# Moving the sum of the rest ahead of the last pieces of w2, and cutting those pieces 7 + 2

## The chip, the cores and the metric

The kernel runs on one core of a Trainium2 chip. The metric is the device time of one execution in microseconds (us), lower is better. Most numbers below come from profiled executions; one such trace covers the span from the first to the last instruction, about 1.8 us less than the device time.

## The reference, cut to what matters

```python
xn = _layernorm(x)                       # x: (2, 1, 576)
return x + attention(xn) @ wo + mlp(xn)

# attention: 32 query heads, 16 kv heads, the last 2048 positions of an 8192-long cache
# mlp: h = relu(xn @ w1 + b1) ** 2 ; out = h @ w2 + b2     w2: (4608, 576)
```

Only two tokens are decoded. The work is therefore reading 53.6 MB of caches and weights once; the weight w2 comes last.

## The kernel before

`D` is 576, `OH` is `D/2`, `OQ` is `D/4`, `B` is 2, `FR` is 9. The rows of w2 come in four groups of nine per partition (one tile each); the last group is cut in two transfers, so there are five pieces. All sums but those of the last group accumulate in `out_ps`, as two halves of 288 columns at partitions 0 and 32. The last group uses another accumulator, `tail_ps`, with four column groups of 144 columns at partitions 0, 32, 64 and 96. What has gathered in `out_ps` ("the sum of the rest") is copied to SBUF and added into `tail_ps` by four f32 matmuls with an identity, between the two last pieces.

```python
    W2P = [(0, 0, 9), (1, 0, 9), (2, 0, 9), (3, 0, 6), (3, 6, 9)]   # group, first row, end row

    def mlp_tail(r0, r1):
        w2_sb = w2_tiles.pop((NG4 - 1, r0))
        if r0 == 0:
            mlp["out"] = psum.tile([P, OQ], F32, tag="misc", name="tail_ps")
        for r in range(r0, r1):
            o = (r - r0) * D
            for i in range(4):
                pe_mm(mlp["out"][32 * i:32 * i + B, :], lhsT=mlp["h"][:, (NG4 - 1) * FR + r, :],
                                 rhs=w2_sb[:, o + i * OQ:o + (i + 1) * OQ], start=(r == 0), stop=(r == FR - 1),
                                 skip_group_check=True, tile_position=(0, 32 * i))
    # ... all of attention ...
    for w in W2P[1:NG4 - 1]:
        mlp_o(*w)                        # second and third piece of w2, into out_ps
    for i in range(2):
        nc.vector.tensor_copy(out=part[:, i * OH:(i + 1) * OH], in_=out_ps[32 * i:32 * i + B, :])
    mlp_tail(*W2P[NG4 - 1][1:])          # 6 rows
    for i in range(4):                   # the sum of the rest
        pe_mm(mlp["out"][32 * i:32 * i + B, :], lhsT=ident_f[0:B, 0:B], rhs=part[:, i * OQ:(i + 1) * OQ],
              start=False, stop=False, skip_group_check=True, tile_position=(0, 32 * i))
    mlp_tail(*W2P[NG4][1:])              # 3 rows

    for i, (cp, eng) in enumerate(((nc.vector.tensor_copy, nc.sync), (nc.scalar.copy, nc.scalar))):
        fin_sb = work.tile([B, OH], BF16, tag="fin", name=f"fin_sb_{i}")
        for q in range(2):
            k = 2 * i + q
            cp(out=fin_sb[:, q * OQ:(q + 1) * OQ], in_=mlp["out"][32 * k:32 * k + B, :])
        eng.dma_start(out=out2d[:, i * OH:(i + 1) * OH], in_=fin_sb[:])
```

## Time and profile before

| what | value |
|---|---|
| device time, three runs | 133.96, 134.13, 134.67 us; median 134.13 |
| span of the trace | 132.3 us |
| main transfer queue | 53.61 MB, 95.0% of its 16 engines' span |
| busiest compute engine | TensorE, 67% |
| third piece of w2 starts on TensorE | 126.07 us |
| last piece of w2 starts on TensorE | 129.17 us |
| final casts start | 129.55 us (VectorE) |

The lines behind this table are shown in the prediction below. They are to be read from the end backwards: find what the last instruction waited for, and go on until something waits for nothing but a transfer. From 126.07 to 129.55 is the only stretch that the change touches. I call those 3.48 us "the interval" throughout: from the start of the third piece's matmuls to the start of VectorE's first final cast.

### The profile page before, as it was taken

Reading aid. Unit: us, or ns where it says so; the run is one execution under the profiler, and the core shown is the slowest. Engines: PE = TensorE matmul, PEld = TensorE weight load, DVE = VectorE, ACT = ScalarE, POOL = GpSimd, SP = SyncE. Lnnn points to the kernel's source line nnn. Section 1 sums busy time; section 2 is a strip of 40 time slices with the busy share of each in tenths; the row PEclk is TensorE's granted clock in tenths of the full one; section 3 lists DMA queues with packets and bytes.
Section 4 is the critical chain, followed back from the end, with each engine's and each line's share of the span. In section 5 each row is a group of like instructions: output and inputs, shape, how many; then the busy total and the mean of one; then the engine's idle time right before and its main releaser. Section 6 shows DMA issues by size and latency. Waiting matters only on the chain.

```text
span 132.3 us, 2040 instructions
## 1 busy us (share of the span) xinstructions
PE 89.0 (67%) x830; PEld 54.4 (41%) x830; DVE 59.6 (45%) x151; ACT 43.9 (33%) x63; POOL 7.7 (6%) x26
## 2 busy tenths in 40 slices
PE   0069319689862957699479989389703996499761
PEld 0059202629521355466174466064403661155430
DVE  6944400224640018555915685827730458644021
ACT  2716400015710136737236447145300651200001
POOL 7700000001000001010010010000010000000000
PEclk9999995955999599999968999977975699869999
DMA  4999989999998999999999999999999999999950
GB/s 139 394 461 468 423 381 431 436 466 514 414 401 352 436 416 451 416 446 426 426 431 426 436 421 443 416 435 431 432 436 426 431 433 439 411 420 429 421 230 1
DMA packets 3632, 53.74 MB, mean 406 GB/s; under 512 B 412, under 2 KB 420, under 8 KB 680
## 3 DMA queue, kind: packets, MB, share of 16 engines
q1 hardware_dynamic: 3604, 53.61, 95.0%
q8 instruction: 6, 0.10, 0.3%
q10 hardware_dynamic: 20, 0.01, 0.0%
q14 instruction: 2, 0.02, 0.0%
HBM read 53.62 MB, written 0.00 MB: 405 GB/s over the span
## 4 chain that ended last, share of the span: by engine, by line
DMA 70%; PE 22%; DVE 2%; ACT 2%; issue 1%; SPq 1%; DVEq 0%; ACTq 0%
DMA k<-in_A_k_cache_dram 42%; DMA w<-in_B_w_dram 14%; DMA wq_sb<-in_A_wq_dram 13%; PE kT_ps L86 11%; PE sc_ps L83 4%; PE q_ps L83 3%; PE pv_ps L83 2%; PE qs_ps L83 1%; DVE kT L286 1%; ACT kT L284 1%; ACT pr L323 1%; PE sm L83 1%; DVE qrow L250 1%; SPq L105 0%; DVE qz L266 0%
## 5 line engine op out<-in xcount | busy, mean ns | idle before, releaser
L86 PE MATMUL kT_ps<-ident_f,k 128*128 128x128 f32 x256 | 41.1, 317 | 12.4 <-DMA k<-in_A_k_cache_dram 11.8
L284 ACT COPY kT<-kT_ps 128x1024 bf16<-128x1024 bf16 x32 | 31.9, 1011 | 36.0 <-PE kT_ps L86 35.7
L86 PEld LDWEIGHTS kT_ps<-ident_f,k 128*128 128x128 f32 x256 | 34.0, 164 | 21.7 <-issue 18.2
L286 DVE COPY kT<-kT_ps 128x1024 bf16<-128x1024 bf16 x32 | 22.1, 691 | 31.5 <-PE kT_ps L86 31.4
L83 PE MATMUL sc_ps<-kT,qz 128*32 128x512 bf16 x128 | 10.5, 414 | 4.6 <-DVE kT L286 2.8
L83 PE MATMUL pv_ps<-v,pT 128*32 128x512 bf16 x128 | 11.9, 440 | 1.0 <-DVE acc L358 0.8
L312 POOL PARTITION_ALL_REDUCE gmax<-m x8 | 2.9, 366 | 103.1 <-DVE m L310 103.1
L323 ACT ACTIVATE pr<-sc_ps,nb 128x512 bf16<-128x512 f32 x8 | 5.5, 687 | 8.3 <-DVE nb L320 8.3
L83 PEld LDWEIGHTS <-xnT 128*4 128x4 bf16 x90 | 3.0, 110 | 12.0 <-issue 11.6
L83 PE MATMUL q_ps<-wq_sb,xnT 128*4 128x512 bf16 x36 | 3.8, 603 | 4.7 <-DMA wq_sb<-in_A_wq_dram 4.7
L308 DVE TENSOR_REDUCE mx<-sc_ps 128x1 f32<-128x512 f32 x8 | 5.5, 683 | 3.1 <-PE sc_ps L83 3.1
L83 PEld LDWEIGHTS <-qz 128*32 128x32 bf16 x128 | 2.3, 98 | 10.1 <-DVE kT L286 6.2
L83 PE MATMUL h_ps<-w_sb,xnT 128*4 128x384 bf16 x54 | 4.1, 443 | 3.2 <-DMA w_sb<-in_B_w_dram 3.2
L358 DVE SCALAR_TENSOR_TENSOR mix<-pv_ps,own_j,mix 128x128 f32<-128x128 f32 x16 | 5.6, 351 | 0.6
L564 ACT CAST fin_sb<-tail_ps 2x144 bf16<-2x144 f32 x2 | 0.5, 272 | 15.8 <-PE tail_ps L83 15.8
L329 DVE STREAM_TRANSPOSE pT<-pr 128x512 bf16<-128x512 bf16 x8 | 5.6, 703 | 0.2 <-ACT pr L323 0.2
L86 PE MATMUL pro_ps<-ident,xs 2*128 2x2 bf16 x10 | 0.6, 165 | 7.6 <-DVE xs L180 7.6
L83 PEld LDWEIGHTS <-pT 128*32 128x32 bf16 x128 | 2.9, 99 | 6.1 <-issue 3.7
L83 PE MATMUL out_ps<-wo_sb,ws 128*2 128x288 bf16 x64 | 5.0, 318 | 0.3 <-DVE ws L387 0.3
L83 PE MATMUL sm<-acc,tohead 128*64 128x129 f32 x16 | 3.7, 315 | 1.8 <-DVE acc L358 1.8
L83 PE MATMUL out_ps<-w,hT_sb 128*2 128x288 bf16 x54 | 3.8, 286 | 1.3 <-DMA w<-in_B_w_dram 1.3
L431 DVE TENSOR_TENSOR hs<-hT_ps,hodd 128x20 f32<-128x20 f32 (+1 forms) x4 | 0.5, 172 | 9.2 <-ACT hodd L428 9.2
(77 smaller groups left out, 58.2 us busy)
## 6 DMA issues: line engine op xcount, KB each, us to landing
k<-in_A_k_cache_dram SPq DMA_DIRECT2D x8, 2048.0 KB, 7.7
v<-in_A_v_cache_dram SPq DMA_DIRECT2D x8, 2048.0 KB, 18.1
w_sb<-in_B_w_dram SPq DMA_DIRECT2D x1, 5184.0 KB, 19.1
wq_sb<-in_A_wq_dram SPq DMA_DIRECT2D x1, 4608.0 KB
wo_sb<-in_A_wo_dram SPq DMA_DIRECT2D x2, 2304.0 KB
w<-in_B_w_dram SPq DMA_DIRECT2D x3, 1296.0 KB, 25.7
w<-in_B_w_dram SPq DMA_DIRECT2D x1, 864.0 KB
w<-in_B_w_dram SPq DMA_DIRECT2D x1, 432.0 KB
```

Source lines behind the costliest of these rows:

```text
L83: return tc.keep_in_program_order(nc.tensor.matmul(out, **kw))
L86: return tc.keep_in_program_order(nc.tensor.transpose(**kw))
L250: nc.vector.tensor_copy(out=qrow[:, 0, :], in_=q_ps[0][0:RB, :])
L284: pin(nc.scalar.copy(out=dst, in_=src))
L286: pin(nc.vector.tensor_copy(out=dst, in_=src))
L308: pin(nc.vector.tensor_reduce(out=mx[:], in_=sc_ps, axis=AX.X, op=ALU.max))
L312: nc.gpsimd.partition_all_reduce(gmax[:], m2[:], channels=P, reduce_op=ReduceOp.max)
L323: pin(nc.scalar.activation(out=pr[:], in_=sc_ps, func=ACT.Exp, bias=nb[:], scale=scale, accum_out=acc[:, Dh:Dh + 1]))
L329: pin(nc.vector.transpose(out=pT[:].rearrange("p t m -> p (t m)"), in_=pr[:]))
L358: op = nc.vector.scalar_tensor_tensor(out=nx, in0=pv_ps[:, j, :], scalar=own_j[:, j:j + 1], in1=acc, op0=ALU.mult, op1=ALU.add)
L431: nc.vector.tensor_tensor(out=hs[:].rearrange("p (g r) b -> p r g b", g=NG4)[:, r0:r0 + n, g:g + 2, :], in0=even[:, :, g:g + 2, :], in1=od ...
L564: cp(out=fin_sb[:, q * OQ:(q + 1) * OQ], in_=mlp["out"][32 * k:32 * k + B, :])
```

## The change

The intent is to shorten what TensorE has to do once the last bytes are there. The sum of the rest enters first and opens the accumulators, its two copies run side by side on VectorE and ScalarE, and the last group of w2 is cut so that only two rows, eight matmuls, come behind the last landing.

```diff
@@ mlp_tail
-        if r0 == 0:
-            mlp["out"] = psum.tile([P, OQ], F32, tag="misc", name="tail_ps")
...
-                                 rhs=..., start=(r == 0), stop=(r == FR - 1),
+                                 rhs=..., start=False, stop=(r == FR - 1),
@@
-    W2P = [(0, 0, 9), (1, 0, 9), (2, 0, 9), (3, 0, 6), (3, 6, 9)]
+    W2P = [(0, 0, 9), (1, 0, 9), (2, 0, 9), (3, 0, 7), (3, 7, 9)]
@@
-    for i in range(2):
-        nc.vector.tensor_copy(out=part[:, i * OH:(i + 1) * OH], in_=out_ps[32 * i:32 * i + B, :])
-    mlp_tail(*W2P[NG4 - 1][1:])
+    for i, cp in enumerate((nc.vector.tensor_copy, nc.scalar.copy)):
+        cp(out=part[:, i * OH:(i + 1) * OH], in_=out_ps[32 * i:32 * i + B, :])
+    mlp["out"] = psum.tile([P, OQ], F32, tag="misc", name="tail_ps")
     for i in range(4):
         pe_mm(mlp["out"][32 * i:32 * i + B, :], lhsT=ident_f[0:B, 0:B], rhs=part[:, i * OQ:(i + 1) * OQ],
-              start=False, stop=False, skip_group_check=True, tile_position=(0, 32 * i))
+              start=True, stop=False, skip_group_check=True, tile_position=(0, 32 * i))
+    mlp_tail(*W2P[NG4 - 1][1:])
     mlp_tail(*W2P[NG4][1:])
```

More of the change, by code (lines that the diff above doesn't have):

```diff
@@ L452, in mlp_tail @@
                 pe_mm(mlp["out"][32 * i:32 * i + B, :], lhsT=mlp["h"][:, (NG4 - 1) * FR + r, :],
-                                 rhs=w2_sb[:, o + i * OQ:o + (i + 1) * OQ], start=(r == 0), stop=(r == FR - 1),
+                                 rhs=w2_sb[:, o + i * OQ:o + (i + 1) * OQ], start=False, stop=(r == FR - 1),
                                  skip_group_check=True, tile_position=(0, 32 * i))
```

## The prediction

> **What bounds the kernel now.** I read the page first for the overall balance, then the chain that ended last, then the last microseconds in order of time, then short windows of the transfer rate.
>
> The page of the kernel before has the busy shares, the slices of the DMA engines and the sum for the queue:
>
> ```profile
> PE 89.0 (67%) x830; PEld 54.4 (41%) x830; DVE 59.6 (45%) x151; ACT 43.9 (33%) x63; POOL 7.7 (6%) x26
> DMA  4999989999998999999999999999999999999950
> q1 hardware_dynamic: 3604, 53.61, 95.0%
> ```
>
> The reader is to see that no compute engine is above 67% of the span, while the main DMA queue fills 95.0% of what its 16 engines could work, at 90% or more in nearly every slice. The program is a stream of 53.61 MB, and an order of instructions can only matter where the stream has ended and something still follows it. So everything that this change can do lies after about 126 us of a span of 132.3 us.
>
> The chain that ended last, asked for its final 30 us (start, length, what):
>
> ```profile
> 110.00 19.13 DMA w<-in_B_w_dram
> 129.13 0.04 issue
> 129.17 0.46 PE tail_ps L83 x12
> 129.63 0.04 ACT fin_sb L564
> ```
>
> The last transfer of w2 lands at 129.13, and from there the chain goes through the twelve matmuls of the last three rows (3 rows x 4 column groups), then the two casts and the output. The four matmuls that add the sum of the rest are not on the chain, nor is its copy by VectorE.
>
> The order of time for the same stretch (start, length, engine, line, operation, and in brackets the idle time before it and what ended it):
>
> ```profile
> 126.07 1.27 PE L83 MATMUL out_ps<-w,hT_sb 128*2 128x288 bf16 x18 [1.32 <-DMA w<-in_B_w_dram]
> 127.37 0.93 DVE L553 COPY part<-out_ps 2x288 f32<-2x288 f32 x2 [5.90 <-PE out_ps L83]
> 128.13 0.55 PE L83 MATMUL tail_ps<-w,hT_sb 128*2 128x144 bf16 x24 [0.80 <-DMA w<-in_B_w_dram]
> 128.60 0.42 PE L83 MATMUL tail_ps<-part,ident_f 2*2 2x144 f32 x8
> 129.17 0.36 PE L83 MATMUL tail_ps<-w,hT_sb 128*2 128x144 bf16 x12
> 129.55 0.62 DVE L564 CAST fin_sb<-tail_ps 2x144 bf16<-2x144 f32 x2 [1.26 <-PE tail_ps L83]
> 129.62 0.57 ACT L564 CAST fin_sb<-tail_ps 2x144 bf16<-2x144 f32 x2 [15.78 <-PE tail_ps L83]
> ```
>
> Three arrivals show as starts of TensorE: the third piece of w2 at 126.07, the 6-row piece at 128.13, the 3-row piece at 129.17. Six rows took 128.13 - 126.07 = 2.06 us, which is 0.34 us a row; three rows took 129.17 - 128.13 = 1.04 us, which is 0.35 us a row. So the arrivals are paced by the rate of the transfer alone. The part that the change wants out of the way, the f32 matmuls, ran from 128.60 to 129.02 and was over 0.11 us before the last piece had landed (129.13). This is the decisive reading: that work is already hidden, though by a thin margin.
>
> Windows of the last stretch (window; length, then busy time of PE, PEld, DVE, ACT, POOL; clock; DMA share; GB/s):
>
> ```profile
> 126.00:126.50 0.50, 0.43 (x8) 0.33 (x9) 0.00 (x0) 0.00 (x0) 0.00 (x0) 1.00 0.97 380
> 127.50:128.00 0.50, 0.00 (x0) 0.00 (x0) 0.47 (x2) 0.00 (x0) 0.00 (x0) 1.00 0.39 159
> 128.50:129.00 0.50, 0.50 (x20) 0.15 (x9) 0.00 (x0) 0.00 (x0) 0.00 (x0) 1.00 0.06 21
> 129.00:129.50 0.50, 0.36 (x16) 0.19 (x12) 0.00 (x0) 0.00 (x0) 0.00 (x0) 1.00 0.00 0
> ```
>
> The DMA share falls from 0.97 to 0.39 and 0.06 before the last landing: most of the 16 engines have run dry and a few late ones finish. The granted clock is 1.00 in all four windows, so the throttle needs no account here.
>
> **What the Trainium skill says.** "DMA: Bandwidth & Descriptors", section "Why a DMA increments its semaphore by 16 and not by 1", says that the engines of one transfer finish independently and that only the full count of 16 means that all its data has landed. The trace agrees: the tail of the share shows stragglers, and TensorE starts its last group only after 129.13. What decides is therefore how many bytes the slowest engine has to move in total, and a new cut of the same last nine rows does not change that.
>
> "TensorE: Matmul & The Clock Gate", Part 3, section "The mechanism", has matmuls on different tiles of the array overlapping, so that each further one adds only its start offset. The trace agrees in kind: one matmul of a row and column group lasts 225 ns, yet 24 of them span 0.55 us and 12 span 0.36 us, an offset of (0.55 - 0.225)/23 = 14 ns and (0.36 - 0.225)/11 = 12 ns. The page's own offset of about 4 ns is not what is seen here; I use 12 to 14.
>
> "VectorE: DVE Perf Modes", in the section on the TRN2 errata, gives a copy from PSUM to SBUF as 120 cycles plus one per element at 0.96 GHz for VectorE and 172 plus one per element at 1.2 GHz for ScalarE. For 288 elements on VectorE that is 425 ns against 447 in the trace; for 144 elements on ScalarE it is 263 ns against 272. For the new ScalarE copy of 288 elements I take the traced 272 ns plus 144/1.2 = 120 ns: an estimate of 0.39 us.
>
> "PSUM — Partial Sum Buffer", section "PSUM bank collisions raise a hardware error", asks that two engines on one bank be kept apart by bank and quadrant of 32 partitions. The two halves of the sum lie at partitions 0 and 32, so they may be copied at once. In the trace the two final casts do just that on one buffer, from 129.55 to 130.17 and from 129.62 to 130.19.
>
> **The change part by part.** In order of time, with the duration of each from the rows above:
>
> The copy. Before, two VectorE copies of 447 ns one after the other, 127.37 to 128.30. After, one on each engine: VectorE from 127.37 to 127.82, ScalarE from about 127.4 to 127.83 (estimate of 0.39 us and a start 0.04 to 0.07 us later, as in the final casts). The sum is ready at about 127.83 instead of 128.30: 0.47 us earlier. None of it was on the path.
>
> The f32 matmuls. The same eight rows of the trace (four matmuls of two passes each), 0.42 us. They move from 128.60 to about 127.88 and end at 128.30, in a stretch where TensorE sat idle for 0.80 us waiting for data. They open the accumulators now. Worth to the end: nothing, as they were over before 129.13 anyway.
>
> The first of the two pieces has 7 rows. It should land one row later, at 128.13 + 0.35 = 128.48, which is after the f32 matmuls' end by 0.18 us. Its 28 matmuls take 0.225 + 27 x 0.014 = 0.60 us, to 129.08; TensorE has started the last of them at 128.86, so it is free when the last piece lands.
>
> The last piece has 2 rows. It ends at the same total of bytes, so it should land at 129.13 as before. Eight matmuls follow instead of twelve: 0.225 + 7 x 0.012 = 0.31 us instead of 0.36. This is the only term on the path: 4 x 12 to 14 ns, about 0.05 us.
>
> What follows is untouched: two casts on each engine (0.62 and 0.57 us) and the output of 1.1 KB on each of two queues. The instruction order of the other engines is the same in both builds up to this point; only ScalarE gains one copy and VectorE loses one.
>
> Sum: 0.00 (copy) + 0.00 (f32 matmuls) + 0.00 (landing) - 0.05 (four matmuls fewer) = -0.05 us, and 134.13 - 0.05 = 134.08. That is 0.04%.
>
> **The rivals.** First, TensorE rather than the transfer could be what holds the last group. For it: between the end of the f32 matmuls (129.02) and the start of the last group (129.17) lie only 0.15 us, so in an execution where the stragglers come earlier, the f32 matmuls would be on the path. Against it: the chain names the landing at 129.13, and three rows in 1.04 us fit the rate of the six rows before. If it were so, the change would gain up to 0.15 us more, and give about 133.9.
>
> Second, the smaller last piece could move less efficiently: a row of it is 2 x 1152 = 2304 bytes a partition instead of 3456. For it: smaller packets may cost more a byte. Against it: a line through the two arrivals (2.06 us for six rows, 1.04 us for three) leaves 0.02 us for a piece on its own, and there are two pieces of 128 rows in both kernels, so what the smaller piece loses the larger wins back. If it cost 0.1 us, the result would be 134.2.
>
> Third, the new order makes TensorE take the f32 matmuls before the 7-row piece, so a late ScalarE copy would hold that piece back. For it: ScalarE had been idle for 15.78 us before its final cast, and the matmuls of its half wait for it. Against it: the sum would be ready 0.65 us before the 7-row piece lands, less the 0.42 us of f32 matmuls; after using up those 0.18 us of slack it would have to eat another 129.13 - 128.86 = 0.27 us before the last group suffered. It would take a copy of over 0.8 us. I expect no cost; if it happened, 134.3.
>
> Fourth, and largest in size: the scatter of the stream itself. The three runs of before lie at 133.96, 134.13 and 134.67, a spread of 0.71 us, more than ten times the effect. A median of a few runs of the changed kernel can fall on either side of 134.13 for that reason alone.
>
> **The range and the chances.** The middle is 134.08, shaded to 134.06 because the first rival can only gain. Downward, the first rival's 0.15 us and a median that falls 0.2 us low give about 133.7; upward, the scatter seen between the middle and the highest run (0.54 us) counts in part, which gives 134.45. Two per cent is 2.68 us. The whole stretch from the landing of the third piece to the end is 132.3 - 126.07 = 6.2 us, and 3.1 us of it are waiting for bytes that both kernels move; I see no way to gain or lose 2.68 us there. So within 2% gets 0.98.
>
> **What would show each step right or wrong.** Right: in the order of time, one part copy on each engine side by side, ending at about 127.8 when counted on this trace's scale; the eight f32 rows begin within 0.1 us of it and end before the 7-row piece starts TensorE; that piece is 2.4 us behind the third piece, the 2-row piece 0.7 us behind it; the last group spans about 0.31 us; the chain still goes from the transfer of w2 through eight matmuls to the casts. The interval from the third piece's start to the start of the casts is 129.55 - 126.07 = 3.48 us before and should be 3.43 after. Wrong: if that interval shrinks by over 0.15 us, TensorE and not the transfer was binding; if the 2-row piece comes over 3.2 us after the third piece, cutting has a cost; if the 28 matmuls have not started when the last piece lands, the copy has become the wait. A span that moves by more than 0.3 us with this interval unchanged would be the stream before 126 us, not the change.

## The result, and the profile after

The changed kernel takes 134.01 us in the median of six runs (133.95 to 134.37), against 134.11 us for six runs of the kernel before. The ratio is 0.9992, with a 95% interval from 0.9972 to 1.0013: the same. Ratios here are the mean time of one kernel's fast runs over that of the other's of the same rounds, so they are not quite the ratio of the medians that I quote.

The page of the kernel after, the lines that answer to those of before:

```profile
PE 89.0 (67%) x830; PEld 54.7 (41%) x830; DVE 59.1 (45%) x150; ACT 44.2 (33%) x64; POOL 7.7 (6%) x26
DMA  4999989999998999999999999999999999999950
q1 hardware_dynamic: 3604, 53.61, 95.2%
```

VectorE (DVE) has one instruction fewer and ScalarE (ACT) one more; the stream is the same.

The chain that ended last, its end (start, length, what):

```profile
109.99 19.10 DMA w<-in_B_w_dram
129.09 0.04 issue
129.13 0.40 PE tail_ps L83 x8
129.53 0.05 ACT fin_sb L563
```

It goes through the same transfer as before. Behind it stand eight matmuls and 0.40 us to the casts instead of twelve and 0.46 us.

The same stretch in order of time (start, length, engine, line, operation; in brackets the idle time before and what ended it):

```profile
126.00 1.27 PE L83 MATMUL out_ps<-w,hT_sb 128*2 128x288 bf16 x18 [1.15 <-DMA w<-in_B_w_dram]
127.30 0.45 DVE L551 COPY part<-out_ps 2x288 f32<-2x288 f32 x1 [5.73 <-PE out_ps L83]
127.33 0.39 ACT L551 COPY part<-out_ps 2x288 f32<-2x288 f32 x1 [13.50 <-PE out_ps L83]
127.80 0.42 PE L83 MATMUL tail_ps<-part,ident_f 2*2 2x144 f32 x8 [0.54 <-DVE part L551]
128.43 1.00 PE L83 MATMUL tail_ps<-w,hT_sb 128*2 128x144 bf16 x36 [0.20 <-DMA w<-in_B_w_dram]
129.46 0.63 DVE L563 CAST fin_sb<-tail_ps 2x144 bf16<-2x144 f32 x2 [1.71 <-PE tail_ps L83]
```

The copies lie side by side, the f32 matmuls end at 128.22, and TensorE still waits 0.20 us for the 7-row piece at 128.43. This view merges both pieces into one line of 36 matmuls; the chain gives the start of the last eight as 129.13. The interval is 129.46 - 126.00 = 3.46 us, against 3.48 before.

The windows of the last stretch (window; length, busy time of PE, PEld, DVE, ACT, POOL; clock; share of the DMA engines; GB/s):

```profile
127.50:128.00 0.50, 0.20 (x8) 0.10 (x8) 0.25 (x1) 0.22 (x1) 0.00 (x0) 1.00 0.39 154
128.50:129.00 0.50, 0.50 (x28) 0.38 (x28) 0.00 (x0) 0.00 (x0) 0.00 (x0) 1.00 0.03 9
129.00:129.50 0.50, 0.33 (x12) 0.10 (x7) 0.04 (x1) 0.00 (x0) 0.00 (x0) 1.00 0.00 0
```

The f32 matmuls (x8) now run in a window in which TensorE was wholly idle before, while the share of the transfers falls away just as it did.

### The profile page after: what moved, and what is told of

Same layout as the page of the kernel before. It is cut to its first block, busy times and chain, and to the rows that moved or that the text cites. A ratio compares the mean times of both kernels' runs of the same rounds, so it can differ in the third digit from the quotient of the medians.

```text
span 132.2 us, 2040 instructions
## 1 busy us (share of the span) xinstructions
PE 89.0 (67%) x830; PEld 54.7 (41%) x830; DVE 59.1 (45%) x150; ACT 44.2 (33%) x64; POOL 7.7 (6%) x26
## 4 chain that ended last, share of the span: by engine, by line
DMA 72%; PE 20%; DVE 2%; ACT 2%; issue 1%; SPq 1%; DVEq 0%; ACTq 0%
DMA k<-in_A_k_cache_dram 44%; DMA w<-in_B_w_dram 14%; DMA wq_sb<-in_A_wq_dram 13%; PE kT_ps L86 10%; PE sc_ps L83 4%; PE q_ps L83 3%; PE pv_ps L83 2%; PE qs_ps L83 1%; DVE kT L286 1%; ACT kT L284 1%; ACT pr L323 1%; PE sm L83 1%; DVE qrow L250 1%; SPq L105 0%; DVE qz L266 0%
```

## The experiments

Every kernel was run six times and traced in one of those runs. The theory: the last landing of w2 sets the end ("landing theory"), the sum of the rest was hidden already, and only matmuls behind the landing count. The main rivals: TensorE and its f32 matmuls held the last group; cutting has a cost; the copy takes the place of the wait.

One thing about the runs has to be said first, because it changes how they must be compared. The 50 runs of the kernel before that were made beside these experiments fall into two groups with nothing between: 34 runs from 133.91 to 134.29 us, mean 134.09, and 16 runs from 134.54 to 134.77 us, mean 134.65. Both count as fast, so the medians and ratios mix them. I call them the lower and the upper group, and compare like with like where I can.

| kernel | median us | its six runs, us | ratio to before | interval us | clock in the tail of the trace |
|---|---|---|---|---|---|
| before | 134.13 | (50 runs, above) | | 3.48 | 1.00 |
| after | 134.01 | 133.95 to 134.37 | 0.9992 | 3.46 | 1.00 |
| after, again | 134.07 | 133.93 to 134.24 | 0.9991 | 3.46 | 1.00 |
| order only | 134.70 | 134.08, 134.21, then 134.69 to 134.82 | 1.0015 | 4.13 | 0.50 |
| cut only | 134.29 | 134.26 to 134.36, and 135.19 | 1.0008 | 3.64 | 1.00 |
| copy undone | 134.47 | 133.94, 133.97, 134.17, then 134.76 to 134.81 | 1.0005 | 4.01 | 0.50 from 129.0 |
| copy doubled | 135.54 | 134.89, then 135.41 to 135.76 | 1.0084 | 4.76 | 0.50 from 130.0 |
| no sum | 134.26 | 134.10 to 134.34 | 1.0000 | 3.58 | 0.50 from 129.0 |
| one piece | 134.91 | 134.45 to 135.18 | 1.0047 | 3.85 | 1.00 |
| 8 and 1 | 134.02 | 133.96 to 134.09, and 134.67 | 0.9992 | 3.52 | 1.00 |
| fewer bytes | 133.64 | 133.33 to 133.46, then 133.82 to 134.02 | 0.9958 | 3.19 | 0.50 from 128.5 |
| one cast | 134.39 | 134.24 to 134.42, and 134.81 | 1.0011 | not comparable | 0.50 |
| order only, filled | 134.19 | 134.05 to 134.23, and 134.62 | 0.9994 | 3.49 | 1.00 |
| after, filled | 134.16 | 134.03 to 134.33 | 0.9991 | not comparable | 1.00 |

### Each part alone

The new order alone: the changed kernel with `(3, 0, 6), (3, 6, 9)` and both copies on VectorE.

```diff
-    for i, cp in enumerate((nc.vector.tensor_copy, nc.scalar.copy)):
-        cp(out=part[...], in_=out_ps[...])
+    for i in range(2):
+        nc.vector.tensor_copy(out=part[...], in_=out_ps[...])
-    W2P = [..., (3, 0, 7), (3, 7, 9)]
+    W2P = [..., (3, 0, 6), (3, 6, 9)]
```

> The new order alone: the sum of the rest goes in first, but the pieces stay at 6 and 3 rows and both copies stay on VectorE. The interval is counted from the start of the third piece of w2 on TensorE to the start of VectorE's final cast: 3.48 us in the kernel before, 3.46 us after. Landing theory (the last landing of w2 sets the end, the sum was hidden already): 3.48 us, within 0.05, and the same time as before within 0.1 us. Rival (TensorE and its f32 matmuls held the last group): the order alone brings the gain, interval 3.33 us or less.

Neither theory foresaw what came: an interval of 4.13 us, and four of six runs in the upper group. The order of time of its trace:

```profile
126.06 1.27 PE L83 MATMUL out_ps<-w,hT_sb 128*2 128x288 bf16 x18 [1.66 <-DMA w<-in_B_w_dram]
127.86 1.12 PE L83 MATMUL tail_ps<-part,ident_f 2*2 2x144 f32 x8 [0.54 <-DVE part L551]
128.91 1.25 PE L83 MATMUL tail_ps<-w,hT_sb 128*2 128x144 bf16 x36
130.19 0.63 DVE L563 CAST fin_sb<-tail_ps 2x144 bf16<-2x144 f32 x2 [1.90 <-PE tail_ps L83]
```

and two of its windows (columns as above, the clock is the third number from the right):

```profile
127.00:127.50 0.50, 0.32 (x6) 0.00 (x0) 0.14 (x1) 0.00 (x0) 0.00 (x0) 1.00 0.64 263
128.00:128.50 0.50, 0.50 (x6) 0.09 (x4) 0.28 (x1) 0.00 (x0) 0.00 (x0) 0.50 0.39 159
```

The third piece starts at 126.06, just as in the kernel before (126.07): the stream is on time. But the granted clock has fallen to 0.50 and the 36 matmuls take 1.25 us without a wait in front of them. TensorE, not the landing, sets the end of this execution. The two runs of the lower group (134.08 and 134.21) are where the landing theory put them. Its tail at full clock was seen later, in the filled version below. (The f32 matmuls' 1.12 us are not all lost to the clock: the second half of them waits for the second copy.)

The new cut alone: the kernel before with 7 and 2 rows.

```diff
-    W2P = [..., (3, 0, 6), (3, 6, 9)]
+    W2P = [..., (3, 0, 7), (3, 7, 9)]
```

> The new cut alone: 7 and 2 rows, but the sum of the rest still between the two pieces and both copies on VectorE. Landing theory with the slack read from the traces: the 28 matmuls start 2.43 us after the third piece; the f32 matmuls begin 0.47 us plus four offsets of 14 ns later, last 0.42 us, and the last group can begin only about 0.95 us after the 28 began, at 3.38 us instead of 3.13: interval about 3.70 us, some 0.2 us longer than before, so the parts need each other. Theory that the landing alone counts, whatever TensorE does before: 3.43 to 3.46 us. Time: 134.3 against 134.05.

```profile
128.44 0.61 PE L83 MATMUL tail_ps<-w,hT_sb 128*2 128x144 bf16 x28 [1.16 <-DMA w<-in_B_w_dram]
128.98 0.42 PE L83 MATMUL tail_ps<-part,ident_f 2*2 2x144 f32 x8
129.34 0.29 PE L83 MATMUL tail_ps<-w,hT_sb 128*2 128x144 bf16 x8
```

At full clock, the f32 matmuls now run from 128.98 to 129.40, past the time at which the last piece lands in the changed kernel (129.13 there). The last group starts at 129.34, after TensorE's own work and not after a transfer; the chain of this trace runs from the 7-row landing through 44 TensorE instructions. The interval is 3.64 us, near the 3.70 expected and 0.16 longer than before. Five of six runs lie at 134.26 to 134.36, about 0.2 us above the lower group of before. So the rival "TensorE holds the last group" is wrong for the kernel before, but only by a thin slack: moving one row into the earlier piece is enough to make it true. That slack is more than the 0.11 us between the end of the f32 matmuls and the landing. Here the last group starts 129.34 - 128.98 = 0.36 us after the first f32 matmul and does not wait for the last to end. By that measure it could have started at 128.60 + 0.36 = 128.96 in the kernel before, 0.21 us ahead of its start at 129.17 (an estimate). The cut needs the order.

The copy back on one engine:

```diff
-    for i, cp in enumerate((nc.vector.tensor_copy, nc.scalar.copy)):
-        cp(out=part[...], in_=out_ps[...])
+    for i in range(2):
+        nc.vector.tensor_copy(out=part[...], in_=out_ps[...])
```

> The changed kernel with the copy back on VectorE alone, two in a row. The sum is ready 0.45 us later (1.30 + 0.9 + 0.05 = 2.25 us after the third piece instead of 1.80), the f32 matmuls run beside the landing of the 7-row piece, whose matmuls start some 0.2 us later than 2.43. Landing theory: TensorE still has handed out the 28 matmuls just before the last piece lands at 3.13 us, so interval 3.46 us within 0.05. Rival (the split copy is what the change needed): interval longer by 0.2 to 0.45 us.

The three runs of its lower group, 133.94, 133.97 and 134.17, are as fast as the changed kernel, which is what the landing theory expects. The traced run was one of the upper group (134.76 us): its clock fell to 0.50 by 129.0, and the interval of 4.01 us is that of a halved clock. No trace shows it at full clock, so its times carry this point, not its interval. One thing stays open: of the 12 runs of the two kernels with the new order and both copies on VectorE (this one and the new order alone) seven were in the upper group, and of 12 of the changed kernel none. They were made in different rounds and not all on one chip, so it is not shown that the second copy engine is what avoids it.

The copy made four times as long:

```diff
-    for i, cp in enumerate((nc.vector.tensor_copy, nc.scalar.copy)):
-        cp(out=part[...], in_=out_ps[...])
+    for i in (0, 1, 0, 1):
+        nc.vector.tensor_copy(out=part[...], in_=out_ps[...])
```

> The changed kernel with the copy made four times as long: both halves on VectorE, each copied twice, 4 x 0.447 us. The sum is ready 1.34 us later than in the changed kernel. Landing theory with a slack of about 0.47 us: the end moves by about 0.87 us, interval about 4.3 us, time about 134.9 us (0.65% slower than before). If the copy's whole delay were on the path: 1.34 us, interval 4.8 us. If the end hung on the landing alone: 3.46 us.

```profile
128.99 0.80 PE L83 MATMUL tail_ps<-part,ident_f 2*2 2x144 f32 x8 [1.58 <-DVE part L551]
129.72 1.17 PE L83 MATMUL tail_ps<-w,hT_sb 128*2 128x144 bf16 x36
```

The interval came out at 4.76 us, on its face the answer "all of the delay counts". But the clock fell in mid-tail here too: it was 0.85 in the window from 129.5 and 0.50 from 130.0, so that the 36 matmuls took 1.17 us instead of the 0.73 us that the trace of one piece, below, has at full clock. (The f32 matmuls' 0.80 us instead of 0.42 are another matter: they ran at clock 1.00, and their second half waited for the last copy, which ended at 127.44 + 1.88 = 129.32.) I work out, as an estimate for full clock: 129.72, when the 36 matmuls start, plus 0.73 us for them and 0.03 us to the casts (both from one piece). That gives casts at 130.48 and an interval of 4.34 us. The fastest run, 134.89 us, fits that: 0.8 us above the lower group of before. The copies ended 3.18 us after the third piece's start instead of 1.75, which is 1.43 us later, and of these 4.34 - 3.46 = 0.88 us reach the end. So the slack is about 0.5 us (0.47 was expected), supported by one run and an estimate and not measured cleanly. What is plain is that a copy that comes late enough does reach the end.

### The bound for hiding the sum

A wrong result: no copy, no f32 matmuls, the 7-row piece opens the accumulators.

```diff
-    for i, cp in enumerate((nc.vector.tensor_copy, nc.scalar.copy)):
-        cp(...)
     mlp["out"] = psum.tile([P, OQ], F32, tag="misc", name="tail_ps")
-    for i in range(4):
-        pe_mm(mlp["out"][...], lhsT=ident_f[0:B, 0:B], rhs=part[...], start=True, stop=False, ...)
@@ mlp_tail
-                start=False
+                start=(r == 0)
```

> A wrong result on purpose: the changed kernel without the copy and without the f32 matmuls, so the sum of the rest never enters. It is the bound for anything that hiding the sum could give. Landing theory: interval 3.46 us within 0.05 and the time of the changed kernel within 0.1 us. Rival (some of the sum is still on the path): shorter by up to the 0.42 us of the f32 matmuls.

Its times are 134.10 to 134.34 us, ratio 1.0000: with the sum gone altogether, nothing is gained. In its trace the clock fell at the end (0.71 in the window from 128.5, then 0.50), so the 36 matmuls took 1.12 us and the interval was 3.58 us, a little more than expected and no less. A slow clock could have hidden a gain in these numbers; the start of the 36 matmuls, still at clock 1.00, settles it:

```profile
128.50 1.12 PE L83 MATMUL tail_ps<-w,hT_sb 128*2 128x144 bf16 x36 [1.17 <-DMA w<-in_B_w_dram]
```

They wait for the transfer and start 128.50 - 126.07 = 2.43 us behind the third piece, exactly as in the changed kernel (128.43 - 126.00). The rival that part of the sum is still on the path is excluded.

### What stands behind the landing, and the landing itself

The last nine rows as one piece:

```diff
-    W2P = [..., (3, 0, 7), (3, 7, 9)]
+    W2P = [..., (3, 0, 9)]
-    mlp_tail(*W2P[NG4][1:])
```

> The changed kernel with the last nine rows as one transfer. It measures what matmuls behind the last landing cost. Landing theory: the landing stays at 3.13 us behind the third piece, then 36 matmuls, 28 more than after, at 13 to 14 ns each: +0.38 us, interval about 3.84 us, time about 134.4 us. If a cut costs the transfer something per piece, the landing comes earlier than 3.13 us by that cost. If matmuls behind the landing cost nothing, interval 3.46 us.

```profile
126.12 1.27 PE L83 MATMUL out_ps<-w,hT_sb 128*2 128x288 bf16 x18 [0.41 <-DMA w<-in_B_w_dram]
129.21 0.73 PE L83 MATMUL tail_ps<-w,hT_sb 128*2 128x144 bf16 x36 [0.87 <-DMA w<-in_B_w_dram]
129.97 0.63 DVE L562 CAST fin_sb<-tail_ps 2x144 bf16<-2x144 f32 x2 [2.10 <-PE tail_ps L83]
```

The trace is at full clock and hits the number: 3.85 us for 3.84. The one piece starts 3.09 us behind the third piece; 6 and 3 landed 3.10 us behind it and 7 and 2 3.13 us behind it, in both traces of the changed kernel. So a cut costs the last landing at most some 0.03 us. The 36 matmuls span 0.73 us, on average (0.73 - 0.225)/35 = 14 ns for each after the first. Their single starts in the trace are uneven: the four matmuls of a row start 3 to 4 ns apart (129.213, 129.216, 129.220, 129.223), and the next row starts 62 ns after the first (129.275). What stands behind the landing is thus counted in rows of 62 ns; in the trace of the new order alone, at clock 0.50, a row takes 120 ns. The median of 134.91 us is above the 134.4 expected: only the fastest run, 134.45, is there, and the traced one, 134.60, is close. With 36 matmuls behind the landing, an execution at a lower clock would lose more, but none of the slower runs was traced.

One step further, 8 rows and 1 row:

```diff
-    W2P = [..., (3, 0, 7), (3, 7, 9)]
+    W2P = [..., (3, 0, 8), (3, 8, 9)]
```

> One step further than the change: 8 rows and 1 row. Landing theory: the 8-row piece lands at about 2.78 us behind the third piece, its 32 matmuls take 0.44 us to hand out, to about 3.22 us, which is past the last landing at 3.13 us, so TensorE takes over as the bound: interval 3.22 + 3 x 0.013 + 0.225 + 0.04 = about 3.50 us, no better than 7 and 2 (3.46 us). If only matmuls behind the landing counted: 3.41 us. Time the same as after within 0.1 us either way.

```profile
109.89 18.71 DMA w<-in_B_w_dram
128.61 0.04 issue
128.65 0.84 PE tail_ps L83 x36
```

The chain now goes to the landing of the first of the two pieces, and TensorE runs all 36 matmuls in one go: it has become the bound. The interval of 3.52 us is what was expected (3.50), and 134.02 us is the time of the changed kernel. Between 7 and 2 and 8 and 1 the bound thus passes from the landing to TensorE; a finer cut gives nothing.

Fewer bytes, a wrong result: two of the nine rows are neither loaded nor multiplied.

```diff
-    W2P = [..., (3, 0, 7), (3, 7, 9)]
+    W2P = [..., (3, 0, 5), (3, 5, 7)]
-                stop=(r == FR - 1)
+                stop=(r == FR - 3)
```

> A wrong result on purpose: the last two rows of each partition of w2 are neither loaded nor multiplied; the remaining seven come as 5 and 2 rows. Landing theory: the last landing comes two rows earlier, 2.43 us behind the third piece instead of 3.13, with eight matmuls behind it: interval 2.76 us, time shorter by 0.70 us, about 133.3 us. Rival (the end is set by TensorE or by something fixed after the stream): less than 0.35 us shorter.

Three runs lie at 133.33 to 133.46 us, mean 133.41, which is 134.09 - 133.41 = 0.68 us under the lower group of before: the expected 0.70. In these three the time follows the bytes; none of them was traced. The other three, 133.82 to 134.02, include the traced one (133.92), whose clock was 0.73 in the window from 128.0 and 0.50 from 128.5. There TensorE was the bound, and the interval was 3.19 us instead of 2.76.

### The scatter of the changed kernel, and a try behind the landing

The changed kernel again, unaltered:

> The changed kernel unaltered, for the scatter of its interval and time: interval 3.46 us within 0.05, time the same as before within 0.2%.

The interval was 3.46 us again and the time 134.07 us, ratio 0.9991 with a 95% interval from 0.9974 to 1.0008.

One cast for all column groups:

```diff
+    nc.vector.memset(mlp["out"][:], 0.0)                        # earlier, in a wait of VectorE
...
-    (two casts on VectorE, two on ScalarE, one transfer for each half of the columns)
+    top = 32 * 3 + B
+    nc.vector.tensor_copy(out=fin_sb[0:top, :], in_=mlp["out"][0:top, :])
+    for b, eng in enumerate((nc.sync, nc.scalar)):
+        eng.dma_start(out=out2d[b].rearrange("(g n) -> g n", g=4), in_=fin_sb[b:top:32, :])
```

> Something behind the landing, which both kernels pay: the result of the four column groups is cast by one VectorE instruction over 98 partitions instead of two by two on each of two engines, and written out by one transfer for each batch row with a step of 32 partitions. The accumulators are zeroed ahead, in a stretch where VectorE waits. Landing theory: everything behind the landing counts in full, so the second cast's 0.3 us goes off the path: about 133.7 us, 0.25% faster than before. Rival (the output's fixed cost or its eight short runs of 288 bytes swallow it): no faster than 133.95 us.

```profile
129.91 0.31 DVE L562 CAST fin_sb<-tail_ps 98x144 bf16<-98x144 f32 x1 [1.99 <-PE tail_ps L83]
130.25 0.66 SPq L564 DMA_DIRECT2D out_dram<-fin_sb  x1
130.25 0.61 ACTq L564 DMA_DIRECT2D out_dram<-fin_sb  x1
```

The cast did go down to 0.31 us, from 0.63 for two. But each output transfer now took 0.66 and 0.61 us to issue, against 0.34 and 0.26 in the changed kernel, and the span ended 133.0 - 130.25 = 2.75 us after the start of the issue instead of 132.2 - 130.11 = 2.09. That is 0.66 us lost for 0.32 us won. Five of the six runs, 134.24 to 134.42, are some 0.3 us above the changed kernel, as this sum says. The rival was right. The transfers of one batch row write four runs of 288 bytes where those of a half wrote two of 576. The Trainium skill, "DMA: Bandwidth & Descriptors", section "Specifications", puts the least size for full rate at 512 bytes; whether it was the size, the number of runs or the step of 32 partitions was not separated here.

### The two groups of runs

What separates the lower from the upper group was still open, and it is larger (0.56 us between the means) than anything the change does. In every trace but one the third piece starts between 125.89 and 126.18 us, in executions of 134.0 as of 134.8 us; the exception is the changed kernel filled, whose fillers stand in front. So the difference does not come from the stream up to there.

The clock records of the traces show more. In each of the 14 traces all changes of the clock lie on a grid of steps of 3.413 us, and where this grid lies against the stream differs from one execution to the next, over the whole step. In seven traces a grid point lies between 127.9 and 128.8 us, and in five of these the clock fell to 0.50 there: one cast and the new order alone (127.97 and 127.94 us), fewer bytes (128.23), copy undone (128.58) and no sum (128.71). In the other two, before (128.53) and after (128.76), it stayed at 1.00. In the seven traces without a grid point there, its fall in the tail came at 129.85 us (copy doubled) or later. So the place of the grid goes with whether the tail runs at half clock, and it is the likely source of the two groups, though that is argued from 14 executions and not tested. Two limits: no execution of the kernel before was traced in its upper group, and no sum, where the clock fell late, took 134.26 us and is not a slow run. What has to happen before a grid point for the clock to fall is not shown. In the step before it TensorE was busy 1.35 us in the new order alone, 1.67 us in before, where the clock stayed, and 1.83 us in copy undone, where it fell.

The last two kernels put six unread matmuls into TensorE's waits.

```diff
-    for w in W2P[1:NG4 - 1]:
-        mlp_o(*w)
+    mlp_o(*W2P[1])
+    fill(4)             # matmuls of 128x128 by 128x512 into an unread PSUM tile
+    mlp_o(*W2P[2])
+    fill(2)
```

The new order alone, filled:

> The kernel of the new order alone, with six matmuls of 512 columns whose result nobody reads: four in TensorE's wait for the third piece, two in its wait for the copy. The traces so far split by the granted clock: where it stayed at 1.00 to the end the times are near 134.0 to 134.3, where it fell to 0.50 between 127.5 and 129 the times are 134.7 to 134.8; the new order alone was over 134.5 in 4 of its 6 runs, the kernel before in 12 of 39. Clock theory (an idle TensorE lets the clock fall in the tail, and the f32 and bf16 matmuls then outlast the landing): clock 1.00 through 129.5, no run over 134.5, median 134.1. Rival (the slow runs come from the stream, and the clock only goes with it): runs over 134.5 as often as before.

```profile
126.10 1.27 PE L83 MATMUL out_ps<-w,hT_sb 128*2 128x288 bf16 x18 [0.88 <-DMA w<-in_B_w_dram]
127.90 0.89 PE L83 MATMUL tail_ps<-part,ident_f 2*2 2x144 f32 x8
128.72 0.85 PE L83 MATMUL tail_ps<-w,hT_sb 128*2 128x144 bf16 x36
129.59 0.62 DVE L571 CAST fin_sb<-tail_ps 2x144 bf16<-2x144 f32 x2 [1.27 <-PE tail_ps L83]
```

```profile
128.00:128.50 0.50, 0.43 (x6) 0.09 (x4) 0.33 (x1) 0.00 (x0) 0.00 (x0) 1.00 0.32 131
```

The same instructions as in the trace of the new order alone, now at clock 1.00: an interval of 3.49 us instead of 4.13, so the fallen clock cost that execution 0.64 us, and the times of the two traced runs differ by 134.75 - 134.20 = 0.55 us. That is about the distance between the groups. It also shows the new order alone at full clock as expected, 3.48. The landing still sets its end: the 36 matmuls take 0.85 us because the last twelve start only at 129.21, after the last landing at 129.17; that is 3.11 us behind the third piece, where the changed kernel has 3.13. (The f32 matmuls' 0.89 us here contain the wait for the second copy.) Whether the fillers keep the clock up is not shown: one of six runs was still in the upper group, against four of six without them, and six runs do not tell these apart. In this trace the grid points were at 127.42 and 130.84; no trace, filled or not, lost its clock in the tail at a grid point before 127.9, so the fillers need not be the reason.

The changed kernel, filled:

> The changed kernel with the same six matmuls, as the version that might beat both. Clock theory: clock 1.00 through 129.5, interval 3.46 us, no run over 134.4, median 134.05, so 0.1% below the mean of the kernel before, whose mean contains its slower runs. If the fillers stand in the way of the third piece's matmuls where it comes early: up to 0.2 us slower than the changed kernel.

No run was over 134.33 us and the trace kept 1.00, but the median of 134.16 us is no better than the changed kernel's. In its trace the fillers made the third piece start at 126.31, about 0.2 us late; the last group still started at 129.13 and the casts at 129.45, so the slack swallowed it. It does not beat the changed kernel, which had no run in the upper group in 12 without any fillers. The kernel before had 16 in 50. By chance alone that would come about in some 2 of 100 drawings of 12 runs from the 62; but I looked for it afterwards, and 8 and 1, with the same order and split copy, had one run of six at 134.67. Whether the change makes the upper group rarer stays open.

## Why the prediction was right, point by point

The time: 134.06 predicted, 134.01 and 134.07 measured in two sets, inside the range, with a ratio that cannot be told from 1. A forecast of no change at all would have fitted the times as well; that the reasons were right shows only in the traces, and there the term that was to be gained is present and tiny.

The copy was to end 0.47 us sooner and win nothing. It ended 1.75 us after the third piece's start instead of 2.23. The f32 matmuls that wait for it started 0.50 us after the copies began (127.80 - 127.30), where the two copies in a row had taken 0.93 us; the ScalarE copy took 389 ns for the estimate of 0.39 us (the ScalarE formula of the Trainium skill, "VectorE: DVE Perf Modes", in the section on the TRN2 errata, gives (172 + 288)/1.2 = 383 ns, also an estimate); and the lower runs with the copy undone are no slower.

The f32 matmuls were to move into an idle stretch and win nothing. They ended 0.21 us before the 7-row piece started, and leaving them out gained nothing.

The landing was to stay. It came 3.13 us behind the third piece instead of 3.10. The second rival's cost of a smaller piece is therefore at most 0.03 us, less than it would have needed.

Four matmuls fewer were to give 0.05 us. The last group spans 0.30 us (busy time summed over windows of 0.1 us) for 0.36 before, and the chain from the landing to the casts is 0.06 us shorter. Of this the interval kept 0.02 (3.46 for 3.48; 3.43 was predicted), as the landing gave the other 0.03 back. The size was nearly right, but its reading was not: the prediction took 12 to 14 ns as the start offset of one matmul after another and denied that the trace shows the page's 4 ns. The single starts show 3 to 4 ns within a row and 62 ns from row to row, so they agree with the page, and what the change took off the path is one row of 0.06 us.

The first rival, TensorE as the bound, was rightly put aside for the kernel before, and cutting alone showed how near it was: that kernel is 0.16 us worse in the interval. The prediction had worked out the parts' values as a sum of independent terms, 0.00 + 0.00 + 0.00 - 0.05. For the whole that holds; for the parts alone it does not, since the last term is only to be had with the second.

One step was wrong, though it did not move the number: "the granted clock is 1.00 in all four windows, so the throttle needs no account here", and the fourth rival's "scatter of the stream itself". The traces of the variants show that the clock can fall to 0.50 in the tail while the stream is on time, and that this makes a difference of about the size of the one between the groups (0.64 us of interval in the new order alone). The kernel before was itself never traced in its upper group, so for it this is inferred from the kernels that share its stream. The Trainium skill, "TensorE: Matmul & The Clock Gate", section "HAM oscillation — how this bites in real kernels", describes waits for transfers that let the clock fall to half; I had looked at the clock of one execution and taken it for that of all.

## What to carry to other kernels

Before hiding work at the end of a stream, compare the time at which it is over with the time of the last landing: here it was over 0.11 us earlier, so all that could be gained was the matmuls behind the landing, at 62 ns for each row of four. Where the slack is that thin, parts of a change are not worth the sum of their values; moving a row without moving the f32 matmuls made things worse. And where runs of one kernel fall into two groups wider apart than the effect, look at the granted clock window by window in more than one execution before blaming the transfers.

## What the Trainium skill lacked or had wrong

- "TensorE: Matmul & The Clock Gate", section "HAM oscillation — how this bites in real kernels", gives waits of over about 3.4 us as the rule for where the clock falls. In the trace of the new order alone it fell from 1.00 to 0.50 at 127.94 us, with no wait of TensorE over 1.66 us in the 9 us before it. (The page's next section tells of falls after shorter idle times, but gives no length.)
- No page that I read has the time to issue a small output transfer by the shape of its runs: 0.34 and 0.26 us for two runs of 576 bytes, 0.66 and 0.61 us for four runs of 288 bytes from every 32nd partition.
